# Window attention issued from a job list that a list scheduler in the kernel puts in order

## The chip, the cores and the metric

One core of a Trainium2 chip runs the whole program. The metric is the device time of one execution in microseconds (us); times are medians of several executions on the same chip.

## The reference

```python
scores = scale * np.matmul(q, k.transpose(0, 1, 3, 2))          # q, k, v: 4 x 8 heads x 576 x 64, float32
mask = (rel >= 0) & (rel < window)                              # causal, window = 128
scores = np.where(mask, scores + bias[None], -1000000000.0)     # ALiBi bias
attn = np.exp(scores - np.max(scores, axis=-1, keepdims=True))
x = np.matmul(attn / (np.sum(attn, axis=-1, keepdims=True) + 1e-09), v)   # -> 2304 tokens x 512
h = x @ w_in;  g = h * (1.0 / (1.0 + np.exp(-1.702 * h)));  x = g @ w_out   # first feed-forward net
h = x @ w2_in; g = np.where(h >= 1, h, np.where(h <= -1, 0.0, (h + 1) ** 2 / 4))
out = g @ w2_out                                                # second net; weights are float64
```

## The kernel before

The attention stage comes first; its result stays on chip, transposed, in `xt`. Work is cut into 16 **units** (one batch, two heads). A unit loads q and k (`load_qk`, six DMAs, ten for unit 0) and v (`load_v`, three DMAs), transposes q and k on TensorE in three chunks (`trans_qk`, chunk 2 is 64 rows; its copy out of PSUM is ScalarE's, the others are VectorE's), and makes the scores of five query blocks m = 0 to 4 in three runs (`scores`: m 0 and 1, m 2 and 3, m 4) with 64x64 tiles of the array. VectorE adds the bias and takes the row maximum (L234), ScalarE takes the exponential (L237, nine per unit), VectorE makes the reciprocal of the sums (L245, L246), GpSimd scales (L250). `trans_p` transposes each block of P on TensorE in 128-column chunks, and ScalarE copies it to `pt`: one copy of three chunks for m = 1 to 3 (L265), two copies for the edge blocks m = 0 and 4 (L270 of 64 partitions, L271 of 128). `pv_unit` is 64 matmuls in 64-column tiles into two PSUM buffers of the pool `ps_a`, which `trans_qk` uses too; a ScalarE and a VectorE copy (L294, L295) write `xt`.

Around this, eight half-slices of the first net's weights are converted from float64 in steps (`load_half`: L66 and L76 on ScalarE, L67 to L74 on VectorE, L78 on GpSimd), so that four of sixteen slices lie ready when the first net starts. `split_block` splits `xt` into two float32r parts (L107, L108).

The order of the work is a sorted list of keys: `at(5 * u - 2.87, load_qk, u)` puts the load of unit u at 2.87 fifths of a unit ahead of its scores, and so on. The framework's own scheduler may then still move instructions. Each engine works its queue strictly in the order issued and stops at the first instruction that has to wait. Buffers: q/k raw 3, qk 2, v 2, pt 2, six P buffers; PSUM 2 (`ps_a`), 4 (`ps_s`), 2 (`ps_t`). The two feed-forward nets follow (`ffn`), a dense stream of 128x128 float32r matmuls.

Of the kernel before, what the change touches and what calls it, by code (L numbers as in the profile page):

```python
# [1 line left out]

# [14 lines left out]
SPLIT = 4  # L17
# [5 lines left out]
P = 128  # L23


@with_exitstack
def tile_window_attention_two_ffn(ctx: ExitStack, tc: tile.TileContext, q, k, v, w1_in, w1_out, w2_in, w2_out, out):
# [10 lines left out]
    def f32(ap):  # L38
        return ap.bitcast(F32)
# [18 lines left out]
    def load_half(src, w, i, in_ffn=False):  # L58
        raw = stage.tile([P, 512, 2], I32, tag="raw", name="raw")
        if i == 0:  # L60
            nc.sync.dma_start(out=raw.rearrange("p (c f) t -> p c (f t)", c=KC), in_=src)
        else:
            nc.sync.dma_start(out=raw.rearrange("p f t -> p (f t)"), in_=src)
        lo, hi = raw[:, :, 0], raw[:, :, 1]
        x = stage.tile([P, 512], I32, tag="x", name="x", bufs=2)
        nc.scalar.activation(f32(x), f32(raw)[:, :, 1], AF.Abs)  # L66
        nc.vector.tensor_scalar(  # L67
            out=f32(x), in0=f32(x), scalar1=HI_MIN, scalar2=HI_MAX, op0=ALU.max, op1=ALU.min)
        finish_late()
        nc.vector.tensor_scalar(  # L70
            out=x, in0=x, scalar1=3, scalar2=0x3FFFFFF8, op0=ALU.logical_shift_left, op1=ALU.bitwise_and)
        nc.vector.scalar_tensor_tensor(  # L72
            out=x, in0=lo, scalar=29, in1=x, op0=ALU.logical_shift_right, op1=ALU.bitwise_or)
        nc.vector.scalar_tensor_tensor(  # L74
            out=x, in0=hi, scalar=SIGN_TOP, in1=x, op0=ALU.bitwise_and, op1=ALU.bitwise_or)
        nc.scalar.copy(w[:, 0, i, :], f32(x))  # L76
        if not in_ffn:
            nc.gpsimd.tensor_tensor(out=w[:, 1, i, :], in0=f32(x), in1=f32(w[:, 0, i, :]), op=ALU.subtract)  # L78
            return
        late.append(lambda: nc.vector.tensor_tensor(  # L80
            out=w[:, 1, i, :], in0=f32(x), in1=f32(w[:, 0, i, :]), op=ALU.subtract))

    def load_weights(w_in, w_out, f, w, halves=(0, 1), in_ffn=False):
        for i in halves:
            src = w_out[f * P:(f + 1) * P, :]
            if i == 0:
                src = w_in.rearrange("(c p) f -> p c f", p=P)[:, :, 2 * f * P:2 * (f + 1) * P]
            load_half(src, w, i, in_ffn)
# [5 lines left out]

    def load_w1(f, i):
        if i == 0:
            w1[f] = new_slice(w_a)
        load_weights(w1_in, w1_out, f, w1[f], (i,))
# [14 lines left out]
    with ExitStack() as actx:  # L113
# [9 lines left out]
        ps_a = pool("ps_a", 2, space=PSUM)  # L123
        ps_s = pool("ps_s", 4, space=PSUM)
        ps_t = pool("ps_t", 2, space=PSUM)
# [8 lines left out]
        bias = acon.tile([P, NP, 2, 192], BF16, tag="bias", name="bias")  # L134

        def setup():
            make_identity(nc, ident)
            nc.gpsimd.iota(reli, pattern=[[-1, 256]], base=P, channel_multiplier=1)
# [9 lines left out]
            for j, r in enumerate(HALVES):  # L148
                nc.gpsimd.tensor_copy(band[r, :], mask[r, 64 * j:64 * j + 192])
            for hp in range(NP):  # L150
# [5 lines left out]
        def make_bias(hp):  # L156
            for e in range(2):
                nc.vector.scalar_tensor_tensor(
                    out=bias[:, hp, e, :], in0=rel, scalar=slope[:, hp, e:e + 1], in1=band,
                    op0=ALU.mult, op1=ALU.add)  # L160

        pbuf = [acon.tile([P, 384], F32, tag=f"p{i}", name=f"p{i}") for i in range(6)]
        done = set()

        units = [(b, hp) for b in range(B) for hp in range(NP)]
        NU = len(units)
        NM = 5
        st = [dict() for _ in units]

        def load_qk(u):  # L170
# [16 lines left out]
        def load_v(u):  # L187
# [10 lines left out]
        def trans_qk(u, c):  # L198
# [3 lines left out]
            ps = ps_a.tile([P, 2, 256], F32, tag="a", name="ps_qk")  # L202
            n = 256 if c < 2 else 64
            for i in range(2):
                for t in range(0, n, P):
# [3 lines left out]
                        ident[0:r, 0:r])  # L209
            (nc.scalar.copy if c == 2 else nc.vector.tensor_copy)(  # L210
                d["qk"][:, :, 256 * c:256 * c + n], ps[:, :, 0:n])

        def groups(m):
            return [(e, 2 * m + e, 64 * max(0, 2 - 2 * m - e)) for e in range(2 if m < NM - 1 else 1)]

        def scores(u, ms):
            b, hp = units[u]
            d = st[u]
            ps = [ps_s.tile([P, 2, 256], F32, tag="s", name="ps_s") for _ in range(len(groups(ms[0])))]
            for a, m in enumerate(ms):  # L220
                for e, i, lo in groups(m):
# [5 lines left out]
            sm = d["sm", ms[0]] = st_p.tile([P, 3, 2, 2], F32, tag="sm", name="sm")  # L227
            for a, m in enumerate(ms):
                n = NM * u + m
                assert n < len(pbuf) or n - len(pbuf) in done  # L230
                pt = d["p", m] = pbuf[n % len(pbuf)]
                for e, i, lo in groups(m):
                    x = pt[:, 192 * e + lo:192 * e + 192]
                    nc.vector.tensor_tensor_reduce(  # L234
                        out=x, in0=ps[e][:, a, lo:192], in1=bias[:, hp, e, lo:192], op0=ALU.add, op1=ALU.min,
                        scale=-0.125, scalar=3.0e38, accum_out=sm[:, 0, a, e:e + 1])
                    nc.scalar.activation(  # L237
                        x, x, AF.Exp, bias=sm[:, 0, a, e:e + 1], scale=-1.0, accum_out=sm[:, 1, a, e:e + 1])

        def norm(u, ms):  # L240
            d = st[u]
            sm = d["sm", ms[0]]
            nn = sum(len(groups(m)) for m in ms)
            s = sm.rearrange("p k a e -> p k (a e)")
            nc.vector.tensor_scalar_add(s[:, 2, 0:nn], s[:, 1, 0:nn], 1e-9)  # L245
            nc.vector.reciprocal(s[:, 2, 0:nn], s[:, 2, 0:nn])  # L246
            for a, m in enumerate(ms):
                for e, i, lo in groups(m):
                    x = d["p", m][:, 192 * e + lo:192 * e + 192]
                    nc.gpsimd.tensor_scalar(  # L250
                        out=x, in0=x, scalar1=sm[:, 2, a, e:e + 1], scalar2=1.0, op0=ALU.mult, op1=ALU.mult)

        def trans_p(u, m):
            d = st[u]
            p = d["p", m]
            done.add(NM * u + m)
# [5 lines left out]
            if 0 < m < NM - 1:  # L262
                for c in range(3):
                    nc.tensor.transpose(ps[:, c, :], p[:, 128 * c:128 * c + 128], ident)  # L264
# [236 lines left out]
```

## Time and profile before

| | |
|---|---|
| time, three runs | median 953.44 us (952.15 to 957.61) |
| the profiled execution | 955.39 us, of which its span 953.6 us |
| granted TensorE clock, mean | 0.993 |
| attention stage: start to the first matmul of the nets | 143.55 us |
| PE (TensorE matmul) busy | 933.4 us, 98% of the span |
| DVE (VectorE), ACT (ScalarE), POOL (GpSimd) busy | 542.7, 398.7, 76.7 us |

PEld is the loading of weights into the array, which overlaps with matmuls. Matmuls are pipelined and their ends are modelled, so a busy PE is not PE at its peak. A span in brackets is the idle time before an instruction, with what ended it.

### The profile page before, as it was taken

The numbers are of one execution on the slowest core, as the hardware profiler recorded it, in microseconds if no ns is written. First come the engines' busy times: TensorE is split into PE (matmuls) and PEld (weight loads), VectorE is DVE, ScalarE is ACT, GpSimd is POOL, SyncE is SP. The second block draws the span as 40 slices with busy tenths as digits, with TensorE's granted clock in tenths as the row PEclk, the third lists the DMA queues.
The fourth block names the chain that finished last, engine by engine and source line by source line (L and its number), as shares of the span: only waits on it lengthen the run. The fifth ranks groups of instructions, "written<-read, shape, count | busy, mean of one in ns | idle before, by whom it ended". The sixth has DMA issues, their size and how long they took to land.

```text
span 953.6 us, 15411 instructions
## 1 busy us (share of the span) xinstructions
PE 933.4 (98%) x5904; PEld 816.3 (86%) x5904; DVE 542.7 (57%) x1290; ACT 398.7 (42%) x980; POOL 76.7 (8%) x166
## 2 busy tenths in 40 slices
PE   6999999999999999999999999999999999999998
PEld 3676668889888999998888899989999999999997
DVE  4689868989533323322489899843543544444443
ACT  3799876545323223222344554522322323323322
POOL 3467650000000000000000000000000000000000
PEclk8899999999999999999999999999999999999999
DMA  5578633344200000000034334000000000000000
GB/s 135 119 175 189 161 93 92 131 152 142 96 1 1 1 1 1 1 0 1 1 100 143 111 111 131 36 23 1 34 1 1 34 1 1 34 1 1 34 1 33
DMA packets 83129, 55.31 MB, mean 58 GB/s; under 512 B 59120, under 2 KB 76784, under 8 KB 83056
## 3 DMA queue, kind: packets, MB, share of 16 engines
q1 hardware_dynamic: 82912, 54.21, 19.8%
q8 instruction: 46, 0.75, 0.3%
q14 instruction: 27, 0.22, 0.1%
q10 hardware_dynamic: 144, 0.13, 0.0%
HBM read 48.66 MB, written 5.66 MB: 57 GB/s over the span
## 4 chain that ended last, share of the span: by engine, by line
PE 87%; ACT 4%; DVE 4%; DMA 2%; SPq 1%; issue 1%; POOL 0%; ACTq 0%; POOLq 0%; DVEq 0%
PE ph L350 40%; PE o L413 21%; PE o L411 18%; ACT p L237 3%; PE ps_x L290 3%; PE ps_s L224 2%; PE ps_qk L207 1%; PE ps_t L264 1%; DMA raw<-in_moe_w_out_dram 1%; DMA qkraw<-in_k_dram 1%; DVE x L74 1%; ACT pt L265 1%; DVE x L72 1%; SPq L183 1%; PE ps_t L268 0%
## 5 line engine op out<-in xcount | busy, mean ns | idle before, releaser
L350 PE MATMUL ph<-xs,w 128*128 128x384 f32 (+2 forms) x2112 | 431.1, 353 | 0.0
L350 PEld LDWEIGHTS ph<-xs,w 128*128 128x128 f32 x2112 | 385.2, 188 | 28.6
L413 PE MATMUL o<-w,gs 128*128 128x512 f32 x864 | 215.8, 394 | 0.0
L411 PE MATMUL o<-gs,w 128*128 128x460 f32 (+1 forms) x960 | 214.4, 372 | 0.5 <-DVE gs L364 0.5
L411 PEld LDWEIGHTS o<-gs,w 128*128 128x128 f32 x960 | 180.3, 188 | 21.9 <-DVE gs L364 0.9
L413 PEld LDWEIGHTS o<-w,gs 128*128 128x128 f32 x864 | 161.2, 188 | 30.0 <-ACT gs L363 0.3
L363 ACT CAST gs<-ph 128x384 fp32r<-128x384 f32 (+2 forms) x176 | 89.6, 510 | 164.8 <-DVE ph L361 112.0
L364 DVE TENSOR_TENSOR gs<-ph,gs 128x384 fp32r<-128x384 f32 (+2 forms) x176 | 104.3, 593 | 72.3 <-ACT gs L363 71.5
L360 DVE TENSOR_TENSOR ph<-ph,ga 128x384 f32<-128x384 f32 x96 | 54.2, 566 | 143.6 <-ACT ga L359 143.4
L357 DVE TENSOR_TENSOR ph<-ph,ga 128x460 f32<-128x460 f32 (+1 forms) x80 | 51.4, 643 | 125.5 <-ACT ga L356 125.4
L359 ACT ACTIVATE ga<-ph,half 128x384 f32<-128x384 f32 x96 | 55.8, 582 | 135.3 <-PE ph L350 131.6
L356 ACT ACTIVATE ga<-ph 128x460 f32<-128x460 f32 (+1 forms) x80 | 44.2, 554 | 138.9 <-PE ph L350 138.9
L250 POOL TENSOR_SCALAR p<-p,sm 128x192 f32<-128x192 f32 (+1 forms) x144 | 63.4, 459 | 61.2 <-DVE sm L246 45.1
L237 ACT ACTIVATE p<-p,sm 128x192 f32<-128x192 f32 (+1 forms) x144 | 61.5, 430 | 7.4 <-DVE sm L234 7.0
L66 ACT ACTIVATE x<-raw 128x512 f32<-128x512 f32 x64 | 43.2, 677 | 47.0 <-DMA raw<-in_moe_w_in_dram 22.1
L361 DVE SCALAR_TENSOR_TENSOR ph<-ga,ph 128x384 f32<-128x384 f32 x96 | 53.9, 561 | 2.8
L76 ACT CAST w<-x 128x512 fp32r<-128x512 f32 x64 | 39.3, 617 | 19.5 <-DVE x L74 18.4
L234 DVE CUSTOM_DVE_ANT_0 p<-ps_s,bias 128x192 f32<-128x192 f32 (+1 forms) x144 | 41.6, 329 | 8.4 <-PE ps_s L224 7.6
L74 DVE SCALAR_TENSOR_TENSOR x<-raw,x 128x512 int32<-128x512 int32 x64 | 43.8, 686 | 0.6
L72 DVE SCALAR_TENSOR_TENSOR x<-raw,x 128x512 int32<-128x512 int32 x64 | 43.7, 686 | 0.5
L290 PEld LDWEIGHTS ps_x<-pt,vraw 64*64 64x64 f32 (+1 forms) x1024 | 29.1, 135 | 13.2 <-ACT qk L210 7.3
L290 PE MATMUL ps_x<-pt,vraw 64*64 64x64 f32 (+1 forms) x1024 | 34.6, 227 | 5.5 <-ACT qk L210 5.3
(50 smaller groups left out, 505.6 us busy)
## 6 DMA issues: line engine op xcount, KB each, us to landing
raw<-in_moe_w_in_dram SPq DMA_DIRECT2D x32, 512.0 KB, 3.7
raw<-in_moe_w_out_dram SPq DMA_DIRECT2D x32, 512.0 KB, 3.6
out_dram<-ob SPq DMA_DIRECT2D x17, 256.0 KB, 2.0
vraw<-in_v_dram SPq DMA_DIRECT2D x32, 128.0 KB, 3.2
qkraw<-in_q_dram SPq DMA_DIRECT2D x30, 128.0 KB, 3.5
qkraw<-in_k_dram SPq DMA_DIRECT2D x30, 128.0 KB, 3.4
sp<-part SPq DMA_DIRECT2D x4, 231.0 KB, 3.5
xt<-sp SPq DMA_DIRECT2D x4, 231.0 KB, 3.1
```

The costliest lines, as they stand in the source:

```text
L74: nc.vector.scalar_tensor_tensor(out=x, in0=hi, scalar=SIGN_TOP, in1=x, op0=ALU.bitwise_and, op1=ALU.bitwise_or)
L237: nc.scalar.activation(x, x, AF.Exp, bias=sm[:, 0, a, e:e + 1], scale=-1.0, accum_out=sm[:, 1, a, e:e + 1])
L250: nc.gpsimd.tensor_scalar(out=x, in0=x, scalar1=sm[:, 2, a, e:e + 1], scalar2=1.0, op0=ALU.mult, op1=ALU.mult)
L290: nc.tensor.matmul(x[e][HALVES[j], m, :], vr[rows, kb, HALVES[j]], pt[rows, n, HALVES[j ^ e]], start=(i == first[e]), stop=(i == last[e]), ...
L350: nc.tensor.matmul(ph, w[f][:, a, 0, c * P:(c + 1) * P], xs[r][c][:, b, :], start=(c == 0 and i == 0), stop=(c == KC - 1 and i == 2))
L359: nc.scalar.activation(a, ph, AF.Relu, scale=0.5, bias=half)
L360: nc.vector.tensor_tensor(out=ph, in0=ph, in1=a, op=ALU.max)
L361: nc.vector.scalar_tensor_tensor(out=ph, in0=a, scalar=1.0, in1=ph, op0=ALU.min, op1=ALU.mult)
L363: nc.scalar.copy(gs[:, 0, :], ph)
L364: act_last[0] = nc.vector.tensor_tensor(out=gs[:, 1, :], in0=ph, in1=f32(gs[:, 0, :]), op=ALU.subtract)
L411: nc.tensor.matmul(o[r][m][:, 0:n], w[f][:, a, 1, sl], gs[:, b, :], start=first, stop=last)
L413: nc.tensor.matmul(o[r][m], gs[:, b, sl], w[f][:, a, 1, :], start=first, stop=last)
```

## The change

The attention stage becomes a list of jobs. `jobs` writes down each piece of work with its engine, how long it occupies it, its latency, what it needs, which buffers it takes and gives back, and a key in units. `in_order` runs a list scheduler over them: per engine it looks at the first 12 open jobs in order of key, takes one that can start, preferring a lower key where starts lie within 150 ns, and adds 95 ns where TensorE changes tile shape. The jobs are issued in the order of the resulting starts, under `tc.manual_schedule()`. The steps of a weight half, the bias, the norm and each exponential are jobs of their own. Buffers: raw 4, qk 3, v 3, pt 3, ten P buffers; PSUM as before. For the edge blocks, columns 192 to 255 of each P buffer are cleared once, and two whole 128-column chunks are transposed and copied in one ScalarE copy. The nets' code is the same; their weight conversion keeps its steps.

```diff
+CAPS = dict(raw=4, v=3, qk=3, a=2, s=4, p=10, t=2, pt=3, wraw=2, wx=2)
+KEYS = dict(dma=-3.04, v=-0.71, b=-0.56, q=-0.6, qe=-0.52, s=-0.5, t=-0.3, x=0.08, n=0.67, po=-0.49, pt=0.98, pe=0.72, pv=0.29, xe=0.54)
+STEP, QSTEP, W_AT, W_STEP, XS_AT = 0.243, 0.09, 3.72, 1.69, 28.0
+RUNS = [(0, 1), (2, 3), (4,)]
+SHAPE_SWITCH, SLACK, AHEAD = 95, 150, 12
...
+def jobs(nu, n_heads2, halves, chunks):
...
+            add(("q", u, c), "PE", occ, lat, at("q", c * QSTEP), [("dma", u), ("ident",)] + [("q", u, 0)] * (c > 0),
+                [("a", (u, c))] + [("qk", u)] * (c == 0), [("raw", u)] * (c == 2), "128x128")
...
+                add(("pe", u, m), "ACT", 365 if wide else 260, 510 if wide else 400, at("pe", m * STEP / 2),
+                    [("pt", u, m)], gives=[("t", (u, m))])
+        add(("pv", u), "PE", 1400, 1600, at("pv"), [("dmav", u)] + [("pe", u, m) for m in range(NM)],
+            [("a", (u, 3)), ("a", (u, 4))], [("pt", u), ("v", u)], "64x64")
...
+def in_order(todo, caps):
...
+                t = max([clock[eng]] + [seen[d] for d in j.needs])
+                if j.shape and shape and j.shape != shape:
+                    t = max(t, clock[eng] + SHAPE_SWITCH)
...
+                t = max([t] + [sorted(free[what])[n - 1] for what, n in counts.items()])
+                if first is None or (t <= first[0] + SLACK if j.key < first[1].key else t < first[0] - SLACK):
+                    first = (t, j)
...
-        raw_p = pool("raw_p", 3)
-        qkt_p = pool("qkt_p", 2)
-        v_p = pool("v_p", 2)
-        pt_p = pool("pt_p", 2)
+        raw_p = pool("raw_p", CAPS["raw"])
+        qkt_p = pool("qkt_p", CAPS["qk"])
+        v_p = pool("v_p", CAPS["v"])
+        pt_p = pool("pt_p", CAPS["pt"])
...
+            for p in pbuf:
+                nc.gpsimd.memset(p[:, 192:256], 0.0)
...
-            nc.tensor.transpose(ps[0:64, 1, :], p[:, 128:192], ident)
-            nc.tensor.transpose(ps[:, c, :], p[:, 128 * c:128 * c + 128], ident)
-            nc.scalar.copy(pt[0:64, n + 1, :], ps[0:64, 1, :])
-            nc.scalar.copy(pt[:, n + c, :], ps[:, c, :])
+            for c in chunks_of(m):
+                nc.tensor.transpose(ps[:, c, :], d["p", m][:, P * c:P * c + P], ident)
...
+            nc.scalar.copy(d["pt"][:, 3 * m + c[0]:3 * m + c[-1] + 1, :], d["ps_t", m][:, c[0]:c[-1] + 1, :])
...
-        for key, _, fn, args in sorted(ev, key=lambda e: e[:2]):
-            fn(*args)
-        xs0 = split_block(0, B1[0])
+        with tc.manual_schedule():
+            for _, (what, *args) in in_order(jobs(NU, NP, 2 * SPLIT, KC), CAPS):
+                do[what](*args)
```

What the new order is shows in the built programs. First SP's queue, which issues the loads, at the start (numbers tell units apart). Before, after unit 0's q and k:

```order
L185 DMA qkraw_111<-in_k_dram 64x2x64
L193 DMA vraw_154<-in_v_dram 128x4x64 x2
L195 DMA vraw_154<-in_v_dram 64x2x64
L193 DMA vraw_177<-in_v_dram 128x4x64 x2
L195 DMA vraw_177<-in_v_dram 64x2x64
L183 DMA qkraw_233<-in_q_dram 128x4x64 x2
L185 DMA qkraw_233<-in_q_dram 64x2x64
L183 DMA qkraw_233<-in_k_dram 128x4x64 x2
```

Now:

```order
L317 DMA qkraw_137<-in_k_dram 64x2x64
L315 DMA qkraw_174<-in_q_dram 128x4x64 x2
L317 DMA qkraw_174<-in_q_dram 64x2x64
L315 DMA qkraw_174<-in_k_dram 128x4x64 x2
L317 DMA qkraw_174<-in_k_dram 64x2x64
L315 DMA qkraw_193<-in_q_dram 128x4x64 x2
```

The loads of v of units 0 and 1 stood ahead of unit 1's q and k; they now stand behind the q and k of units 1 and 2.

Then TensorE in the middle of the stage. Before (`ps_s` scores, `ps_qk` 128x64 chunk 2 of q and k, `ps_t` blocks of P, `ps_x` the product with v):

```order
L264 MATMUL ps_t<-ident,p_105 128x128 x3
L207 MATMUL ps_qk<-ident,qkraw 128x128 x3
L224 MATMUL ps_s<-qk 64x64 x2
L224 MATMUL ps_s<-qk 64x128 x2
L224 MATMUL ps_s<-qk 64x192 x4
L264 MATMUL ps_t<-ident,p_106 128x128 x3
L207 MATMUL ps_qk<-ident,qkraw 128x64 x2
L264 MATMUL ps_t<-ident,p_107 128x128 x3
L224 MATMUL ps_s<-qk 64x192 x8
L290 MATMUL ps_x<-pt,vraw 64x64 x32
L268 MATMUL ps_t<-ident,p_108 64x128
L269 MATMUL ps_t<-ident,p_108 128x128
```

Now:

```order
L406 MATMUL ps_t<-ident,p_113 128x128 x3
L406 MATMUL ps_t<-ident,p_114 128x128 x2
L359 MATMUL ps_s<-qk 64x64 x2
L359 MATMUL ps_s<-qk 64x128 x2
L359 MATMUL ps_s<-qk 64x192 x4
L429 MATMUL ps_x<-pt,vraw 64x64 x32
L359 MATMUL ps_s<-qk 64x192 x8
L339 MATMUL ps_qk<-ident,qkraw 128x64 x2
L406 MATMUL ps_t<-ident,p_105 128x128 x2
```

Pieces of one tile shape stand together more often, and here the product with v stands ahead of chunk 2. Over the whole stage TensorE changes between 64-wide tiles (scores and products), the 64-row chunk and the other transposes 133 times before and 95 times now.

Last, VectorE at the end of the stage. Before, from the last score block (`sm_2503`) on:

```order
L234 ISA p1_106,sm_2503<-ps_s_2500,bias_104 128x192
L234 ISA sm_2503 128x1
L245 TENSOR_SCALAR sm_2503<-sm_2503 128x1
L246 RECIPROCAL sm_2503<-sm_2503 128x1
L295 COPY xt2_69<-ps_x_2547 128x4x64
```

Now (`sm_2474`; `x_2531` and `x_2671` are weight halves, the second one of the fifth slice):

```order
L370 ISA p9_114,sm_2474<-ps_s_2473,bias_104 128x192
L370 ISA sm_2474 128x1
L385 TENSOR_SCALAR sm_2381<-sm_2381 128x4
L389 RECIPROCAL sm_2381<-sm_2381 128x4
L199 TENSOR_SCALAR x_2531<-x_2531 128x512
L441 COPY xt2_69<-ps_x_2497 128x4x64
L202 TENSOR_SCALAR x_2531<-x_2531 128x512
L385 TENSOR_SCALAR sm_2474<-sm_2474 128x1
L199 TENSOR_SCALAR x_2671<-x_2671 128x512
L205 SCALAR_TENSOR_TENSOR x_2531<-raw_2100,x_2531 128x512
L389 RECIPROCAL sm_2474<-sm_2474 128x1
```

Between the two steps of the last norm stand two steps of weight conversion.

## Rows read from the trace of the kernel before

**Rows 1.** The page: busy time, share of the span and instructions of each engine.
```profile
PE 933.4 (98%) x5904; PEld 816.3 (86%) x5904; DVE 542.7 (57%) x1290; ACT 398.7 (42%) x980; POOL 76.7 (8%) x166
```
**Rows 2.** Stretches: sum over twelve units, 31.5 to 124.5 us, product to product; busy us.
```profile
sum 93.00, PE 88.22 PEld 64.10 DVE 79.08 ACT 85.16 POOL 57.37; mean PE 7.35 PEld 5.34 DVE 6.59 ACT 7.10 POOL 4.78
```
**Rows 3.** Timeline of PE, attention stage: start, length, instructions merged.
```profile
62.35 0.68 PE L290 MATMUL ps_x<-pt,vraw 128*64 128x64 f32 x14
...
64.65 0.30 PE L268 MATMUL ps_t<-ident,p 128*64 128x128 f32 x1
...
66.17 0.49 PE L264 MATMUL ps_t<-ident,p 128*128 128x128 f32 x3
66.50 0.60 PE L207 MATMUL ps_qk<-ident,qkraw 128*128 128x128 f32 x4
...
68.47 0.55 PE L264 MATMUL ps_t<-ident,p 128*128 128x128 f32 x3
68.95 0.88 PE L224 MATMUL ps_s<-qk 64*64 64x192 f32 x16
69.76 0.34 PE L290 MATMUL ps_x<-pt,vraw 128*64 128x64 f32 x4
...
134.21 2.30 PE L290 MATMUL ps_x<-pt,vraw 128*64 128x64 f32 x64
...
141.74 1.88 PE L290 MATMUL ps_x<-pt,vraw 128*64 128x64 f32 x64
143.55 6.80 PE L350 MATMUL ph<-xs,w 128*128 128x462 f32 x31
```
**Rows 4.** Waits, 32 to 124.5 us: who for whom, us, times, longest.
```profile
ACT p L237 <- DVE sm L234: 4.7, 10, 1.0
PE ps_x L290 <- ACT qk L210: 4.0, 12, 0.7
```
**Rows 5.** Lines of ACT, 31.5 to 124.5 us: busy us, mean ns, idle before.
```profile
L237 ACT ACTIVATE p<-p,sm 128x192 f32<-128x192 f32 (+2 forms) x107 | 45.8, 431 | 5.0 <-DVE sm L234 4.7
...
L66 ACT ACTIVATE x<-raw 128x512 f32<-128x512 f32 x10 | 7.0, 698 | 0.9 <-POOL w L78 0.6 <-DMA raw<-in_moe_w_in_dram 0.2
```
**Rows 6.** Timeline of ACT within one unit.
```profile
65.17 0.42 ACT L294 COPY xt<-ps_x 128x320 f32<-128x320 f32 x1
65.48 0.27 ACT L270 COPY pt<-ps_t 64x128 f32<-64x128 f32 x1
...
65.80 0.64 ACT L76 CAST w<-x 128x512 fp32r<-128x512 f32 x1
66.31 0.47 ACT L237 ACTIVATE p<-p,sm 128x192 f32<-128x192 f32 x1
...
69.72 0.46 ACT L265 COPY pt<-ps_t 128x384 f32<-128x384 f32 x1
70.08 0.26 ACT L210 COPY qk<-ps_qk 128x128 f32<-128x128 f32 x1
70.24 0.48 ACT L265 COPY pt<-ps_t 128x384 f32<-128x384 f32 x1
```
**Rows 7.** Timeline of the start: SP's queue, PE, ACT.
```profile
6.33 1.14 SPq L193 DMA_DIRECT2D vraw<-in_v_dram  x2
...
10.03 1.15 SPq L183 DMA_DIRECT2D qkraw<-in_q_dram  x2
...
16.26 0.66 PE L207 MATMUL ps_qk<-ident,qkraw 128*128 128x128 f32 x2 [1.70 <-DMA qkraw<-in_k_dram]
...
20.24 0.35 ACT L237 ACTIVATE p<-p,sm 128x64 f32<-128x64 f32 x1
...
29.93 0.35 ACT L237 ACTIVATE p<-p,sm 128x64 f32<-128x64 f32 x1 [0.42 <-DVE sm L234]
```
**Rows 8.** Stretches: busy us of PE, PEld, DVE, ACT, POOL; granted clock; DMA.
```profile
16.00:28.00 12.00, 11.60 (x71) 7.35 (x71) 6.15 (x31) 6.12 (x26) 3.57 (x9) 0.50 0.60 135
200.00:240.00 40.00, 40.00 (x193) 36.01 (x193) 38.04 (x70) 20.99 (x38) 0.00 (x0) 1.00 0.43 139
```

More of the change, by code (lines that the diff above doesn't have):

```diff
@@ L1 @@
+from collections import Counter, namedtuple
 from contextlib import ExitStack, nullcontext
+from functools import partial
 import numpy as np
@@ new lines, in in_order @@
+def in_order(todo, caps):
+    queues = {}
+    for j in sorted(todo, key=lambda j: j.key):
+        queues.setdefault(j.eng, []).append(j)
+    clock = dict.fromkeys(queues, 0)
+    free = {what: [0] * n for what, n in caps.items()}
+    seen, shape, order = {}, None, []
+    while any(queues.values()):
+        best = None
+        for eng, queue in queues.items():
+            first = None
+            for j in queue[:AHEAD]:
+                if any(d not in seen for d in j.needs):
+                    continue
+                t = max([clock[eng]] + [seen[d] for d in j.needs])
+                if j.shape and shape and j.shape != shape:
+                    t = max(t, clock[eng] + SHAPE_SWITCH)
+                counts = Counter(what for what, _ in j.takes)
+                if any(len(free[what]) < n for what, n in counts.items()):
+                    continue
+                t = max([t] + [sorted(free[what])[n - 1] for what, n in counts.items()])
+                if first is None or (t <= first[0] + SLACK if j.key < first[1].key else t < first[0] - SLACK):
+                    first = (t, j)
+            if first and (best is None or first[0] < best[0]):
+                best = first
+        t, j = best
+        queues[j.eng].remove(j)
+        clock[j.eng] = t + j.occ
+        seen[j.name] = t + j.lat
+        shape = j.shape or shape
+        for what, _ in j.takes:
+            free[what].sort()
+            free[what].pop(0)
+        for what, _ in j.gives:
+            free[what].append(t + j.lat)
+        order.append((t, j.name))
+    return order
@@ L56, in finish_late, with load_raw @@
             late.pop()()
-    def load_half(src, w, i, in_ffn=False):
+    def load_raw(w_in, w_out, f, i):
         raw = stage.tile([P, 512, 2], I32, tag="raw", name="raw")
         if i == 0:
+            src = w_in.rearrange("(c p) f -> p c f", p=P)[:, :, 2 * f * P:2 * (f + 1) * P]
             nc.sync.dma_start(out=raw.rearrange("p (c f) t -> p c (f t)", c=KC), in_=src)
         else:
[L63 to L81, printed above, removed]
@@ L90, in new_slice, with load_weights @@
+    def load_weights(w_in, w_out, f, w):
+        for i in range(2):
+            raw = load_raw(w_in, w_out, f, i)
+            x = stage.tile([P, 512], I32, tag="x", name="x", bufs=2)
+            for step in range(6):
+                convert(step, raw, x, w, i, nc.vector)
+                if step == 1:
+                    finish_late()
+            late.append(partial(convert, 6, raw, x, w, i, nc.vector))
     def new_slice(pool):
@@ L154, in setup, with do_b, do_dma @@
                         nc.vector.memset(slope[r, hp, e:e + 1], -8.0 * 2.0 ** (-8.0 * (h + 1) / H))
[L156 to L170, printed above, removed]
+        def do_b(hp, e):
+            nc.vector.scalar_tensor_tensor(
+                out=bias[:, hp, e, :], in0=rel, scalar=slope[:, hp, e:e + 1], in1=band, op0=ALU.mult, op1=ALU.add)
+        def do_dma(u):
             b, hp = units[u]
@@ L275, in pv_unit, with do_pv @@
+        def do_pv(u):
             d = st[u]
             pt, vr = d["pt"], d["v"]
-            x = [ps_a.tile([P, 8, 64], F32, tag="a", name="ps_x") for _ in range(2)]
+            x = d["ps_x"] = [ps_a.tile([P, 8, 64], F32, tag="a", name="ps_x") for _ in range(2)]
             todo = []
```

266 lines of the change are left out of this document (175 added, 91 removed).

## The prediction

> **What bounds the kernel now.** The page comes first: PE is busy 98% of the span [rows 1], so whatever the change gives must come out of time in which PE is busy with little or waits. The timeline of PE then shows where the change can act at all. The attention stage runs until the nets' first matmul at 143.55 us [rows 3]; behind that the nets' code and order are the same. So the question is how much earlier that matmul starts.
>
> Inside the stage I read the period of a unit, from one product with v to the next. It is 69.76 - 62.35 = 7.41 us in one of the tightest units, and (134.21 - 31.5) / 13 = 7.90 us as the mean of thirteen [rows 2, 3]: 31.5 is the start of the stretch of rows 2, 134.21 that of a later product. Of twelve units' 93.0 us PE is busy in 88.22 and ACT in 85.16, DVE in 79.08, POOL in 57.37 [rows 2]. Two engines are close to full, and each waits now and then for the other: each product with v waits for ACT's copy of chunk 2 (12 waits, 4.0 us), ACT's exponentials for DVE (4.7 us) [rows 4]. A stage of that sort is bound by neither engine alone but by both and the order in which they meet.
>
> What each engine needs without waits is the floor. **PE:** a product takes 143.55 - 141.74 = 1.81 us when nothing holds it, and 64.65 - 62.35 = 2.30 us in the unit read [rows 3]; without these 0.49 us the unit has 7.41 - 0.49 = 6.92 us of PE work. **ACT:** nine exponentials at 0.431 us, 3.88 [rows 5]; the wide copy 70.08 - 69.72 = 0.36, three of them 1.08; chunk 2, 70.24 - 70.08 = 0.16; the xt copy 65.48 - 65.17 = 0.31; a pair of edge copies 65.80 - 65.48 = 0.32, two pairs 0.64 [rows 6]. Together 6.07 us a unit, without weights. A weight half adds 0.698 (L66) [rows 5] and 66.31 - 65.80 = 0.51 (L76) [rows 6], 1.21 us; eight of them, spread over 16 units, are 0.60 a unit. So ACT has 6.67 us of work in 7.90, PE 6.92; the mean unit waits about 0.98 us on PE.
>
> **The change part by part.**
>
> *Edge copies.* Of each pair one copy of 256 columns remains. 128 columns take 0.16 and 384 take 0.36 [rows 6], so 256 take 0.26: 0.06 saved per pair, 0.12 a unit. ACT's floor falls to 6.55 us. The transposes stay as many; the ten memsets of P buffers lie on POOL ahead of its first scaling, which waits for the first exponentials anyway; if that cover failed they would delay unit 0 alone.
>
> *Order on PE.* There are 38 fewer changes of tile shape. A row of three transposes takes 66.50 - 66.17 = 0.33 us when transposes follow, and 68.95 - 68.47 = 0.48 us when scores follow [rows 3]: 0.15 us for a change. 38 x 0.15 = 5.7 us, 0.36 a unit: PE's floor falls from 6.92 to 6.56 us. I take no more, since the two ends of such a step are alike elsewhere; nothing if the wait were there for another reason.
>
> *Order and deeper buffers together.* Both floors are then near 6.56 us, against a period of 7.90. No row of the old trace shows what the new order leaves in waits. The bounds: none (6.56), or all of today's loss kept (7.90). I take the middle of today's 0.98 us of waits, 0.49, since some of it is of a kind that the new order removes (in the place shown, the product no longer has chunk 2 ahead of it) while each engine still stops at its first waiting instruction: 6.56 + 0.49 = 7.05 us. 13 units x (7.90 - 7.05) = **11.0 us less**.
>
> *Start.* The six DMAs of v for units 0 and 1 occupy SP's queue from 6.33 to 10.03 us [rows 7], ahead of unit 1's q and k. They now come later, so unit 1's last k lands 3.7 us earlier: its transposes, which waited for k until 16.26 [rows 7], can start at 12.56. From there to unit 1's first exponential it was 20.24 - 16.26 = 3.98 us [rows 7]; kept, it starts at 16.5. Up to unit 2's first exponential ACT has by its new order nine exponentials, unit 0's five copies and one chunk 2: 3.88 + 1.08 + 0.52 + 0.16 = 5.64 us, so 22.2. Before it was 29.93 [rows 7], with two copies more done (0.32 + 0.36). **Gain 29.93 - 0.68 - 22.2 = 7.0 us.** The difference to the bare 3.7 us is that PE ran this stretch at a granted clock of 0.50 [rows 8], the 1.2 GHz level, after it had waited for q and k; with the loads 3.7 us earlier the wait is short. Bounds: 3.7 us if the clock still falls, 8.5 us if at 2.4 GHz the 3.98 us shrink to 2.5 too (an estimate: PE's part of it at half length).
>
> SP's queue later: q and k are issued three units ahead, v about two, and a load of v waits for the product three units back with the next q and k queued behind it. With four raw buffers that is 2 units or 14 us of room, so I cost it at nothing; were v late by more, PE would wait for k.
>
> *End.* The last reciprocal stands behind two weight steps on DVE, the first of which waits for an L66 on ACT, and the last copies to pt behind split casts (four, moved here from units 1 to 4, whose 2 us then fall out of the units' periods) and one weight cast. From the rows, between 0 (hidden) and three steps of 0.7 [rows 5]; I take **1.0 us more**, since the chain from the last exponential to the nets is a serial one.
>
> **The sum:** -7.0 - 11.0 + 1.0 = **-17.0 us**. Against the profiled execution, 955.39 - 17.0 = 938.4 (span 936.6); that run lies 1.95 us over the median of the runs, 953.44, so the time I forecast is **936.4 us**. The nets' first matmul would stand at about 126.5.
>
> **The rivals.**
>
> *A, the floor is reached:* 13 x (7.90 - 6.56) = 17.4, start 8.5, end 0: -25.9, **927.5 us**. For it: buffers for a unit more everywhere, and an order made with latencies. Against: two engines equally full, in strict order.
>
> *B, PE is as full as it looks.* If its busy time is real, the units can give no more than PE's idle time, 93.00 - 88.22 = 4.78 us in twelve [rows 2], 5.2 in thirteen: -7.0 - 5.2 + 1.0, **942.2 us**. Against it: the weight loads fill only 64.10 of the 93.00 us [rows 2], and 6.92 us of work in 7.90 were found. The Trainium skill, page "Perfetto Trace Analysis", section "Identifying the Most-Contended Engine", says that matmul busy time is no good measure of TensorE's room and the busy share of LDWEIGHTS is: by it 69% here, room for A or the forecast, by the other 95% and B.
>
> *C, the waits only change their names.* PSUM is as scarce as before (2, 4 and 2 banks), and the wait that repeats in every unit is for a PSUM buffer of `ps_a` [rows 4]. Then the units keep 7.90 us: -7.0 + 1.0, **947.4 us**. The Trainium skill, the same page, section "Optimization Strategy", says that a gap that repeats on the full engine can mean too few SBUF or PSUM buffers; here only SBUF gets more, which by that sentence alone speaks for C.
>
> *D, the clock falls at the start all the same:* -3.7 - 11.0 + 1.0, **939.7 us**; with C together 950.7 us.
>
> *E, slower: ACT stands at each copy of P.* ACT's new order has five copies to pt a unit, fixed between exponentials by the scheduler's own figures, which price a product at 1.4 us where 1.81 is measured and a change of shape at 0.095 where it is 0.15. If PE is late, ACT stops at the copy with ready exponentials queued behind it, and these feed the scaling and so the next transposes. At worst each of the five waits for its transposes' 0.55 us [rows 3]: 6.55 + 2.75 = 9.30 us a unit, 13 x 1.40 = 18.2 more, less 6.0 from start and end: +12.2, **965.6 us**. It decides once ACT's waits pass 7.90 + 6.0 / 13 - 6.55 = 1.8 us a unit. Against it: pt is three deep now and PE's floor no higher than ACT's.
>
> *F, the nets give some back:* DVE is busy 38.04 of 40 us in their opening [rows 8], converting weights, and the new order leaves about one half-slice more to do then, some four steps of 0.7 us [rows 5]: up to 2.8 us of PE's time if nothing covers them, 939.2 us with the forecast's other terms, inside its range.
>
> **How the numbers follow.** Forecast 52% (931 to 942), A 10%, B 13%, C 6%, D 10%, C with D 5%, E 4%. The range of 8 in 10 goes from the floor to C: **927 to 948 us**. A measurement of this kernel can tell about 0.5%, 4.8 us, from no change: faster than 948.6 are the forecast, A, B, C and D, 0.91; within it C with D, 0.05; slower 0.04.
>
> **What would show it.** Right: the nets' first matmul at 124 to 130 us; a mean period near 7.05 between products (they come less evenly, so over ten or more); unit 2's first exponential near 22 us and a granted clock of 1.0 in 16 to 28; no wait of PE on chunk 2 in every unit; PE's busy time still above 90%. Wrong: the period at 7.6 or more with waits of ACT on `ps_t` (E or C), a clock of 0.5 past 20 us (D), or PE waiting inside the nets (F).

## The result, and the profile after

The changed kernel takes 945.56 us (median of four runs, 944.14 to 946.71) against 955.53 us for the kernel before, run beside it on the same chip: a ratio of 0.9896, 95% interval 0.9855 to 0.9938. It is faster by 10.0 us; forecast was 17.0 us. The profiled spans say the same, 953.6 and 943.6 us. The time lies inside the range of the prediction, but the terms of its sum miss by 2 to 6 us each, so each is taken by itself.

The page's line of engines, which answers to [rows 1], tells nothing: PE is as full as before.

```profile
PE 921.8 (98%) x5904; PEld 810.7 (86%) x5904; DVE 546.8 (58%) x1290; ACT 398.2 (42%) x948; POOL 76.7 (8%) x176
```

Four marks cut the program into four stretches: unit 2's first exponential, unit 15's first exponential, the nets' first matmul, the end. An exponential is a better mark than a product with v here, since the new order issues products unevenly. Three rows of the timeline of the changed kernel (start us, length, engine, line, operation):

```profile
20.54 0.35 ACT L378 ACTIVATE p<-p,sm 128x64 f32<-128x64 f32 x1
...
118.23 0.35 ACT L378 ACTIVATE p<-p,sm 128x64 f32<-128x64 f32 x1
...
131.54 0.47 PE L497 MATMUL ph<-xs,w 128*128 128x462 f32 x1
```

In the kernel before the same marks stand at 29.93 [rows 7], 133.07 and 143.55 us [rows 3]. The period below is the time from the first mark to the second, divided by 13.

| stretch | before | after | gain | forecast |
|---|---|---|---|---|
| start, to unit 2's first exponential | 29.93 | 20.54 | 9.4 | 7.0 |
| units 2 to 15, 13 periods | 7.93 each | 7.51 each | 5.4 | 11.0 |
| end, to the nets' first matmul | 10.48 | 13.31 | -2.8 | -1.0 |
| nets | 810.05 | 812.06 | -2.0 | 0 |
| sum | 953.6 | 943.6 | 10.0 | 17.0 |

The stretches of the changed kernel (start:end and length; busy us of PE, PEld, DVE, ACT, POOL with counts; granted clock; DMA share; GB/s) show the start and the nets at once:

```profile
16.00:28.00 12.00, 11.85 (x192) 8.86 (x192) 10.76 (x56) 11.37 (x46) 7.45 (x19) 1.00 0.66 148
31.00:116.00 85.00, 77.28 (x1317) 57.20 (x1316) 71.19 (x325) 76.33 (x294) 49.87 (x106) 1.00 0.71 168
131.00:160.00 29.00, 29.00 (x168) 26.03 (x164) 26.11 (x47) 16.53 (x29) 1.11 (x1) 1.00 0.38 124
160.00:200.00 40.00, 37.75 (x177) 32.77 (x176) 37.09 (x70) 20.54 (x39) 0.00 (x0) 1.00 0.47 144
```

How the 12.0 us ahead of the nets divide among the first three stretches depends on the marks. When unit 2's exponentials begin, the new kernel already runs unit 0's product, the old one has not begun it, so that the 13 periods hold 12 products now and 13 before. By products, the forecast's own mark, the first, the fourteenth and the last stand here:

```profile
31.49 0.34 PE L290 MATMUL ps_x<-pt,vraw 128*64 128x64 f32 x4
19.54 1.81 PE L429 MATMUL ps_x<-pt,vraw 128*64 128x64 f32 x61
...
118.78 1.88 PE L429 MATMUL ps_x<-pt,vraw 128*64 128x64 f32 x64 [0.26 <-DVE xt L441]
...
129.72 1.89 PE L429 MATMUL ps_x<-pt,vraw 128*64 128x64 f32 x64
```

The first row is of the kernel before, the others are of the changed one. The start then gains 31.49 - 19.54 = 12.0 us; the 13 periods behind the first product go from 7.90 to (118.78 - 19.54) / 13 = 7.63 us, 3.5 us less in all; and the last two periods of products lose as much. From the first product to the last it is 110.2 us before and now.

From 16 to 28 us the granted clock is 1.00 where it was 0.50 [rows 8], and PE passes 192 matmuls where it passed 71. From 160 to 200 us PE has 2.25 us without work; in the kernel before it was busy for 39.97 of these 40. The waits of PE say where that is. First those from 31 to 124 us (who for whom: us in total, times, longest), then those behind 131.5 us:

```profile
PE ps_s L359 <- DVE qk L345: 2.5, 3, 0.9
PE ps_t L406 <- POOL p L394: 2.3, 5, 0.7
PE ps_t L406 <- ACT pt L411: 1.3, 3, 0.6
PE ps_x L429 <- DVE xt L441: 0.9, 2, 0.6
PE ps_qk L339 <- DMA qkraw<-in_k_dram: 0.6, 1, 0.6
...
PE o L558 <- DVE part L522: 1.8, 3, 0.6
PE o L558 <- ACT gs L510: 0.5, 1, 0.5
```

The wait of every product for chunk 2 (12 times, 4.0 us [rows 4]) is gone, and 8.0 us of waits under other names have come, of which the five largest are shown. In the nets PE waits for `part`, DVE's copies of a partial sum to be spilled; in the kernel before it had no such wait.

The end is read from DVE's timeline, with PE's last transposes behind it:

```profile
126.76 0.14 DVE L385 TENSOR_SCALAR sm<-sm 128x1 f32<-128x1 f32 x1
126.82 0.58 DVE L199 TENSOR_SCALAR x<-x 128x512 f32<-128x512 f32 x1
127.33 0.68 DVE L205 SCALAR_TENSOR_TENSOR x<-raw,x 128x512 int32<-128x512 int32 x1
127.93 0.14 DVE L389 RECIPROCAL sm<-sm 128x1 f32<-128x1 f32 x1
...
129.35 0.44 PE L406 MATMUL ps_t<-ident,p 128*128 128x128 f32 x2 [0.64 <-POOL p L394]
```

The reciprocal of the last group of rows, 0.14 us of work, starts 1.17 us after its sum, behind two weight steps; the scaling, the last transposes and the last product follow in a chain. That is the term "End", seen as forecast, though at 2.8 us in place of 1.0.

### The profile page after: what moved, and what is told of

The parts are those of the page before. It is cut to its first block, busy times and chain, and to the rows that moved or that the text cites. A ratio compares the mean times of both kernels' runs of the same rounds, so it can differ in the third digit from the quotient of the medians.

```text
span 943.6 us, 15391 instructions
## 1 busy us (share of the span) xinstructions
PE 921.8 (98%) x5904; PEld 810.7 (86%) x5904; DVE 546.8 (58%) x1290; ACT 398.2 (42%) x948; POOL 76.7 (8%) x176
## 4 chain that ended last, share of the span: by engine, by line
PE 85%; DVE 6%; DMA 4%; ACT 2%; SPq 1%; issue 1%; POOL 0%; ACTq 0%; DVEq 0%; POOLq 0%
PE ph L497 39%; PE o L560 21%; PE o L558 19%; PE ps_x L429 2%; DMA raw<-in_moe_w_in_dram 2%; PE ps_s L359 2%; DMA raw<-in_moe_w_out_dram 1%; PE ps_t L406 1%; PE ps_qk L339 1%; DVE x L208 1%; DVE x L205 1%; DVE p L370 1%; DMA qkraw<-in_k_dram 1%; DVE qk L345 1%; DMA sp<-part 1%
## 5 line engine op out<-in xcount | busy, mean ns | idle before, releaser
L406 PE MATMUL ps_t<-ident,p 128*128 128x128 f32 x208 | 36.7, 288 | 5.5 <-POOL p L394 3.9
L213 DVE TENSOR_TENSOR w<-x,w 128x512 fp32r<-128x512 f32 x56 | 38.3, 687 | 2.2 <-ACT w L211 0.6
```

## The experiments

Times are medians, unless a single run is named. Ratios are to the kernel before, on the same chip. The changed kernel's own stage, which stands unchanged up to the last unit in three of the runs below (10 to 12), has periods of 7.54 to 7.60 us there against 7.51, so differences below 0.1 us a period mean nothing. The granted clock has to be read beside the period: from 31 to 116 us it is 1.00 in the change, and 0.88 to 0.98 in all of the runs 3 to 12 but the one with both reliefs (7): PE had stood somewhere in its units, and 0.50 was granted for some microseconds behind it.

### 1. The loads alone, in the old order

```
-        load_v(0)
+        at(-9.2, load_v, 0)
...
-                at(5 * u - 2.87, load_qk, u)
+                at(5 * u - 2.87 if u > 1 else -9.5, load_qk, u)
```

> The kernel before, with unit 1's q and k issued ahead of the v loads of units 0 and 1, and nothing else. Theory: the start's gain is the loads' alone and needs no new order. Unit 2's first exponential moves from 29.93 us to between 21 and 23, the granted clock stays at 1.0 between 16 and 28 us, the units behind keep their 7.93 us, and the kernel becomes 7 to 9 us faster. Rival: the start needs the new order too, since unit 0 and unit 1 are still issued as before; then unit 2's first exponential stays above 25 us and no more than 4 us are gained. Second rival: the clock falls all the same, with a wait one unit later; gain 3.7 us.

Measured: 949.0 us, ratio 0.9934 (0.9913 to 0.9954), 6.7 us less; span 947.9. The timeline of ACT and the stretch from 16 to 28 us:

```profile
22.29 0.35 ACT L237 ACTIVATE p<-p,sm 128x64 f32<-128x64 f32 x1 [0.36 <-DVE sm L234]
```
```profile
16.00:28.00 12.00, 11.58 (x159) 7.65 (x158) 8.44 (x48) 11.18 (x49) 6.39 (x18) 1.00 0.62 139
```

Unit 2's first exponential comes 7.6 us earlier and the clock does not fall: most of the start's gain is the loads' (by products 7.1 of 12.0 us, with unit 0's at 24.41). Behind it the period is 8.03, the end 10.48 us, so 5.7 us of span remain, a little under what was expected. Of the change's 10.0 us more than half is six DMA issues moved.

### 2. Loads, whole edge blocks and deeper buffers, in the old order

```
-        raw_p = pool("raw_p", 3)
+        raw_p = pool("raw_p", 4)
...
-            nc.scalar.copy(pt[0:64, n + 1, :], ps[0:64, 1, :])
-            nc.scalar.copy(pt[:, n + c, :], ps[:, c, :])
+            nc.scalar.copy(pt[:, n + lo:n + lo + 2, :], ps[:, lo:lo + 2, :])
```

(and qk, v and pt to 3, P to ten buffers, the loads as in 1).

> The kernel before with the loads moved, the edge blocks copied whole and all the deeper buffers (raw 4, qk 3, v 3, pt 3, ten P buffers), in the old order. Theory: buffers alone change nothing, since a written order stops at the same instruction whatever lies free; the edge copies give at most 0.12 us a unit. So 0 to 2 us faster than with the loads alone, period 7.8 to 7.93. Rival: the old order waits for buffers, and the depth alone gives a good part of what the change gave in its units (0.42 us each): 4 us or more over the loads alone, period 7.6 or less.

Measured: 954.97 us, ratio 0.9997 (0.9975 to 1.002). Neither theory: 6 us slower than the loads alone. The waits of PE from 10 to 35 us show why at the start:

```profile
PE ps_qk L211 <- DMA qkraw<-in_k_dram: 0.9, 1, 0.9
PE ps_qk L211 <- DMA qkraw<-in_q_dram: 0.8, 1, 0.8
```

On SP's queue unit 2's v now stands ahead of its q and k (issued at 13.70 and from 15.55 us), which a third v buffer allows, and the first mark moves from 22.29 to 23.71 us. The period is 7.98, so the buffers and the edge copies together do not shorten the units in the old order, and the end grows to 14.95 us, where PE waits 1.84 us in the middle of a product and then runs at a granted clock of 0.84 (131 to 160 us). By the medians the changed kernel, with the new order, is 9.4 us faster than this one; the two were not run side by side, and by the profiles 3.2 us of it is this kernel's later start and 1.6 its longer end. The edge copies were not tried alone; whatever they give is hidden in 7.98.

### 3. Six P buffers in the new order

```
-CAPS = dict(raw=4, v=3, qk=3, a=2, s=4, p=10, t=2, pt=3, wraw=2, wx=2)
+CAPS = dict(raw=4, v=3, qk=3, a=2, s=4, p=6, t=2, pt=3, wraw=2, wx=2)
```

> The changed kernel with six P buffers as before instead of ten, in its pool and in the scheduler's list. Theory: P's buffers are the one depth that the new order lives on, since its exponentials run a unit ahead of the transposes; with six the order falls back to at least the old period, 7.9 us or more, and the kernel to 955 us or more. Rival: the order makes the gain and the depth only follows; period 7.6 or less.

Measured, a single run: 979.85 us, period 9.64. (The scheduler counts free P buffers but does not name them. With six, twelve query blocks lose their buffer to a new block before they are transposed, so part of the attention output is wrong.) This does not show the depth by itself. The scheduler makes another order with six, some transposes now stand behind the scores and exponentials of the block that took the buffer (2.0 us of PE's waits from 24 to 150 us, and none in the change), PE stops more often and the granted clock from 31 to 116 us is 0.88. What is shown is that this scheduler with these keys makes no usable order from six; that P's depth is of no use to the old order fits experiment 2, where it was one of several changes. The Trainium skill, page "Perfetto Trace Analysis", section "Optimization Strategy", says that a gap which repeats can mean too few SBUF or PSUM buffers; this run, 2.1 us a unit longer with six P buffers, fits that and cannot tell it from the changed order.

### 4. Truer prices for PE

```
-        add(("pv", u), "PE", 1400, 1600, at("pv"), [("dmav", u)] + [("pe", u, m) for m in range(NM)],
+        add(("pv", u), "PE", 1650, 1850, at("pv"), [("dmav", u)] + [("pe", u, m) for m in range(NM)],
-SHAPE_SWITCH, SLACK, AHEAD = 95, 150, 12
+SHAPE_SWITCH, SLACK, AHEAD = 200, 150, 12
```

> The changed kernel with the scheduler's prices of a product at 1.65 us instead of 1.4 and of a change of tile shape at 0.2 us instead of 0.095, both nearer to the trace; the order changes, the work does not. Theory E': the mispriced PE is why waits of 0.7 us a unit were left; with true prices the copies of P come in their places, the period falls to 7.2 or less and the kernel is 3 to 5 us faster than the change. Rival, theory P: the waits are small beside PE's own work and another order of the same work gives the same period, 7.4 to 7.6, within 1.5 us of the change.

Measured: 955.12 us, ratio 1.0006 (0.999 to 1.0023); period 8.32. (Here too, for two query blocks P is overwritten before it is transposed.) Unit 1's product comes at 44.85 us instead of 27.62, and from 20 to 60 us PE waits 3.7 us for q and k. Neither theory came. The new order puts products off, unit 1's first, and makes them up in two places: the time from first exponential to first exponential is 15.99 us from unit 5 to 6 and 14.22 from 13 to 14, with a granted clock of 0.50 from 41.5 to 51.7 and from 109.7 to 116.6 us, where PE had stopped (the profile is of the fastest of ten runs). The whole is worse with these keys; how much of it is the order and how much the clock was not separated, and whether mispriced PE left the waits (E') stays open.

### 5. No weight steps among the units; 6. less work in the product; 7. both

```
-STEP, QSTEP, W_AT, W_STEP, XS_AT = 0.243, 0.09, 3.72, 1.69, 28.0
+STEP, QSTEP, W_AT, W_STEP, XS_AT = 0.243, 0.09, 30.0, 1.69, 28.0
```
```
+            todo = todo[:9]
             first = [min(i for i, t in enumerate(todo) if t[0] == e) for e in range(2)]
```

The first diff alone:

> The changed kernel with the eight weight halves planned behind all units, so that ACT, DVE and POOL have no weight steps among them; the whole is longer, since the nets then wait for weights. Read is the period of a unit (first exponential of unit 2 to that of unit 15, divided by 13: 7.51 us in the change). Theory Q: PE stands because ACT and DVE deliver late, and their weight steps (1.21 us on ACT and some 2.2 on DVE for each half) take the time; the period falls to 7.1 or less. Theory P: PE's own work with its shape changes is what fills the unit (6.83 us busy in the new trace and more than my floor of 6.56); the period stays at 7.3 or more.

The second alone:

> The changed kernel with 9 of the 16 groups of matmuls in each product with v; the seven groups over the middle block of keys are left out (all but the first query group's), so part of the attention output is missing. PE has 7/16 of 1.65 us, about 0.72 us, less to do in each unit, ACT, DVE and POOL exactly as much as before. Theory P (PE's own work fills the unit): the period falls from 7.51 us by most of the 0.72, to 7.0 or less. Theory Q (ACT and DVE with their weight steps set the pace): the period stays above 7.3 and PE's idle time grows by what it was spared.

Both:

> Both reliefs at once: no weight steps among the units (ACT is spared 0.6 us a unit, DVE 1.1) and 9 of 16 groups of matmuls in each product (PE is spared 0.72; part of the attention output is missing). Alone the first gave a period of 7.41 and the second 7.36, against 7.51. Theory T, two engines that are both near full and meet in a fixed order: relieved together they give about the 0.6 us that neither gave alone, period 6.9 or less. Theory U, order, transfers and buffers set the period and the engines' work does not: 7.2 or more.

Measured, a single run each: 966.35, 943.15 and 961.61 us, of which only the units count. Periods: **7.41** without weight steps, **7.36** with less product, **6.79** with both (first exponentials at 20.72 and 108.97 us). The stretch from 31 to 116 us of the three, in that order:

```profile
31.00:116.00 85.00, 80.40 (x1404) 61.26 (x1402) 57.76 (x311) 72.74 (x290) 39.81 (x103) 0.98 0.58 135
```
```profile
31.00:116.00 85.00, 76.71 (x1070) 55.78 (x1072) 72.33 (x327) 77.05 (x299) 50.89 (x106) 0.96 0.73 171
```
```profile
31.00:116.00 85.00, 80.10 (x1186) 59.13 (x1184) 60.50 (x330) 78.85 (x317) 44.61 (x116) 1.00 0.58 133
```

Relieving ACT (with DVE and POOL) gives 0.10 us a unit, relieving PE by 0.72 gives 0.15, both together 0.72. But the three did not run at the same granted clock: 0.98, 0.96 and 1.00 in these rows. Each single relief has one unit, from first exponential to first exponential, that is longer than the same one of the change: without weight steps the one from 76.94 to 87.78 us, 10.84 us for 8.50; with less product the one from 34.51 to 44.85 us, 10.34 for 8.79. PE stops in each, and the clock falls behind the stop. Without weight steps:

```profile
78.55 2.42 PE L429 MATMUL ps_x<-pt,vraw 128*64 128x64 f32 x61 [2.14 <-DMA vraw<-in_v_dram]
80.00:84.00 4.00, 4.00 (x58) 3.16 (x56) 1.70 (x10) 1.48 (x5) 0.42 (x1) 0.57 0.69 156
```

With less product:

```profile
41.42 0.39 PE L339 MATMUL ps_qk<-ident,qkraw 64*128 64x64 f32 x2 [1.73 <-DVE xt L442]
41.00:45.00 4.00, 3.58 (x17) 2.59 (x18) 3.83 (x21) 3.54 (x14) 0.82 (x2) 0.57 0.74 166
```

Without that one unit, in the run and in the change alike, the two reliefs give 0.31 and 0.29 us a unit, 0.60 together, and both at once 0.72. So P and Q fall, each by the run in which it asked for 7.0 or 7.1: neither side alone sets the pace. T's number came, 6.79, but that the two together give what neither gives alone is not shown; they may simply add, and the stops and the clock that they bring take a part (theory U), as the wait for v here. Each of the three is one profile.

The rows also show what PE's busy time is worth. With less product PE does 0.72 us less in each unit, yet its busy time goes only from 77.28 / 85 x 7.51 = 6.83 to 76.71 / 85 x 7.36 = 6.64 us a unit. That is not the clock alone: from 66 to 116 us, at 1.00 in the change (first row) and with less product (second), it goes from 45.58 / 50 x 7.42 = 6.76 to 45.27 / 50 x 7.20 = 6.52, with the periods of units 8 to 15.

```profile
66.00:116.00 50.00, 45.58 (x780) 33.96 (x778) 42.46 (x195) 45.95 (x178) 31.40 (x64) 1.00 0.68 163
66.00:116.00 50.00, 45.27 (x663) 32.83 (x659) 43.61 (x196) 47.06 (x183) 32.18 (x63) 1.00 0.67 161
```

### 8. Weight loads earlier on SP's queue

```
+def early_loads(order):
+    for h in range(8):
+        i = order.index(("wd", h))
+        before = [j for j in range(i) if order[j][0] in ("dma", "dmav")][-3:]
+        j = max([before[0]] + [order.index(("w4", g)) + 1 for g in [h - 2] if g >= 0])
+        order.insert(j, order.pop(i))
+    return order
```

> The changed kernel with each weight half's load issued three loads earlier on SP's queue and not a row moved on the other engines. In the new trace SP issues without a pause from 49.5 to 75 us and ACT stands 2.9 us at L197 for two weight loads that come late, with exponentials queued behind. Theory S: late transfers take a part of the units; ACT's waits there vanish and the period falls from 7.51 to about 7.3, 2 to 3 us faster than the change. Rival: the time is lost at the next wait instead (q and k then come later by one load, PE waits for k); the period stays within 0.1 us and the time within 1 us of the change's.

Measured: 946.55 us, ratio 0.9915 (0.9886 to 0.9944); period 7.68. ACT's waits for weights are gone, and among PE's waits from 21 to 117 us stands now

```profile
PE ps_qk L348 <- DMA qkraw<-in_k_dram: 1.8, 1, 1.8
```

where it was 0.6 us. The rival's mechanism came: PE waits for k instead. Its time came too, 1.0 us over the change, but not its period, which is 0.17 us longer. That is one unit, from 34.32 to 46.18 us, 11.86 us for 8.79, with the wait for k (36.42 us) and a granted clock of 0.50 behind it from 38.1 to 41.5; the other twelve are 0.07 us shorter on the mean.

### 9. Weight steps and split casts earlier

```
-STEP, QSTEP, W_AT, W_STEP, XS_AT = 0.243, 0.09, 3.72, 1.69, 28.0
+STEP, QSTEP, W_AT, W_STEP, XS_AT = 0.243, 0.09, 3.72, 1.45, 9.0
```

> The changed kernel with the weight halves planned 1.45 instead of 1.69 units apart and the four split casts planned from unit 9 on instead of behind everything. In the new trace the last unit's reciprocal stands 1.2 us behind two weight steps on DVE, and two weight steps on ACT stand ahead of the last exponential. Theory: the stretch from the last unit's first exponential to the nets, 13.3 us now and 10.5 in the kernel before, falls to 11.5 or less, and the units get longer by no more than 0.1 us, since PE fills them: 0.5 to 2.5 us faster than the change. Rival: ACT and DVE set the pace of the units, so that what is taken from the end comes back there, 8 casts of some 0.5 us; within 0.5 us of the change.

Measured: 949.32 us, ratio 0.9938 (0.9919 to 0.9958). The kernel is 3.8 us slower than the change, so neither theory nor rival came. The end falls to 11.91 us, most of the way to the 11.5 expected, and the nets to 809.1, but the period rises to 8.19, 8.8 us in all, for eight split steps of some 0.5 to 0.7 us and one weight half. The order changed everywhere else too, and the granted clock from 31 to 116 us is 0.96; how much is due to each stays open.

### 10. The last weight half behind the last scalings

```
+def late_steps(order):
+    last = [n for n in order if n[0] in ("w0", "w1", "w2", "w3", "w4", "w5", "w6") and n[1] == 7]
+    order = [n for n in order if n not in last]
+    i = order.index(("po", 15, 2, 4, 0)) + 1
+    return order[:i] + last + order[i:]
```

> The changed kernel with the seven steps of the last weight half issued behind the last unit's scalings instead of among its exponentials and reciprocal, all else in the same order. Theory: in the last 13.3 us the serial chain from the last exponential to the nets is held by these steps (0.57 us on ACT ahead of the last exponential, 1.2 us on DVE ahead of the last reciprocal), so the stretch falls to about 12.0 and the kernel is 1.0 to 1.7 us faster than the change. Rival: the weights then come late in the nets, whose DVE is full at their opening, and PE waits there for what was gained here; within 0.5 us of the change.

Measured: 949.63 us, ratio 0.9951 (0.9931 to 0.9971), 4.1 us slower than the change. The end grew to 16.72 us. ACT and PE there (line numbers are 7 higher than the change's):

```profile
132.75 0.62 ACT L218 CAST w<-x 128x512 fp32r<-128x512 f32 x1 [2.26 <-DVE x L215]
133.27 0.57 ACT L466 CAST xs<-xt 128x462 fp32r<-128x462 f32 x1
133.75 0.36 ACT L418 COPY pt<-ps_t 128x256 f32<-128x256 f32 x1
```
```profile
134.16 1.74 PE L436 MATMUL ps_x<-pt,vraw 128*64 128x64 f32 x36 [3.68 <-ACT pt L418]
```

The reciprocal came at once (0.18 us after its sum), but the steps now stood ahead of the last copy to `pt` on ACT: a cast that waited 2.26 us for DVE held it, and PE stood 3.68 us. It is rival E's mechanism, ACT standing in strict order ahead of a copy that PE needs, in one place; the edit was a step short.

### 11. `part` on ACT

```
-                    nc.vector.tensor_copy(part, src[:, 0:n])
+                    nc.scalar.copy(part, src[:, 0:n])
```

> The changed kernel with the four copies of a partial sum to `part` in the first net on ACT instead of DVE. Theory: the 2.0 us that the nets gave back are PE's waits for these copies, because DVE comes to them late with conversions ahead of them; then PE's idle time between 160 and 200 us goes from 2.25 us to under 0.7 and the kernel is about 1.5 to 2 us faster than the change. Rival: it is the conversions themselves that are late, or the spill's transfers that hold the buffer; then PE waits as long behind another name and the time stays within 0.5 us of the change's.

Measured: 943.38 us, ratio 0.9886 (0.9843 to 0.9929). The stretch from 160 to 200 us:

```profile
160.00:200.00 40.00, 39.47 (x189) 35.16 (x189) 36.46 (x67) 21.75 (x41) 0.00 (x0) 1.00 0.48 155
```

PE has 0.53 us without work there instead of 2.25, and the nets take 942.3 - 132.32 = 810.0 us as in the kernel before. The nets' loss was these copies on a late DVE.

### 12. Both ends together

`part` on ACT, and `late_steps` with the steps behind the last copy to `pt` and the split casts:

```
-    i = order.index(("po", 15, 2, 4, 0)) + 1
+    i = max(order.index(("pe", 15, 4)), order.index(("xl", 3))) + 1
```

> The changed kernel with two edits: the copies to `part` on ACT (2.2 us by the run that had it alone), and the seven steps of the last weight half issued behind the last unit's copies of P and the split casts, not among its exponentials and not, as in the run that lost 3.4 us, ahead of its last copy. Theory: the last reciprocal and the last copy both come at once, the stretch from the last unit's first exponential to the nets falls from 13.3 to 11.8 to 12.3 us, the nets take 810 us, and the kernel is 3 to 3.7 us faster than the change, about 942. Rival: DVE, full at the nets' opening, now has seven steps more to do there, PE waits for it at the hidden layer, and only the 2 us of the first edit remain or less: 943.5 to 945.

Measured: 944.63 us, ratio 0.9896 (0.9876 to 0.9917). The end is 12.12 us, 1.2 less, as expected; but the nets take 811.7 us. PE's waits from 110 to 400 us begin with

```profile
PE ph L504 <- ACT w L218: 1.7, 2, 1.6
```

The rival held: the weight steps pushed behind the stage are late for the nets. Of all kernels that do the whole work, the one of experiment 11 has the lowest median, 2.2 us under the change's; the two intervals overlap, and what speaks for it is the 2.1 us that the nets' stretch lost.

## Why the prediction was right or wrong

**Right: the bound, as far as tried.** "Bound by neither engine alone" is what experiments 5 to 7 show. "The order in which they meet" as the rest of it is argued: the changed order moved the waits and did not shorten them.

**Wrong: the size of the units' gain, -11.0 against -5.4 us.** The step that failed is "I take the middle of today's 0.98 us of waits". By the forecast's floors the new order kept all of that loss. With the forecast's floors the period lies 7.93 - 6.92 = 1.01 us over the higher floor before, and 7.51 - 6.56 = 0.95 after; in experiments 5 to 7, with ACT's floor at 5.95 or PE's at 5.84 or both, it lies 0.85, 0.81 and 0.84 over, though the first two hold a unit at a lowered clock, and 0.56 and 0.57 without it. So the loss was kept from the kernel before to the change, and the gain, 0.42 us a unit, is about the floor's fall, 0.36. By products the period is 7.63 us, 1.07 over the floor and a gain of 0.27, which is no better; the nets' first matmul, at 131.54 us, missed the forecast's 124 to 130. The upper bound was set wrong with it: "all of today's loss kept" is 6.56 + 0.98 = 7.54 us, not 7.90. That the floor falls by 38 changes of shape at 0.15 us fits this, but was not tried by itself, and why the loss stays about 1 us is open.

**Edge copies and depth.** 0.12 us a unit for the copies was never seen apart. Deeper buffers give the old order nothing (2); that P's are needed by the new one is likely and not shown apart from the order (3); the depth of raw, qk, v and pt was not tried alone in it.

**Start, -7.0 against -9.4.** The mechanism was right: loads earlier, short wait, clock at 2.4 GHz. Unit 1's transposes start at 11.85 us, where 12.56 was forecast, and from unit 1's first exponential to unit 2's it is 20.54 - 14.86 = 5.68 us, where 5.64 was. The mis-sized term is the one between, 3.98 us "kept": it is 14.86 - 11.85 = 3.01, as only the bound of 8.5 had it. That the old order with the loads moved reaches 22.29, where 22.2 was forecast, is luck: there unit 1's first exponential is earlier (15.60 for 16.5) and the way to unit 2's longer (6.69 for 5.64).

**End, +1.0 against +2.8.** The mechanism was right and undersized: the last reciprocal stands 1.17 us behind its sum. Moving the last half's steps gave 1.2 of it back (12). The rest was not taken apart.

**The rivals.** A did not come. B's number for the units (5.2 us) is close to the 5.4 measured, yet that is luck, for its reason falls: with 0.72 us less work PE's busy time shrank by a third of that or less, so a good part of it was not work. The Trainium skill, page "Perfetto Trace Analysis", section "Identifying the Most-Contended Engine", says that matmul busy time is no good measure of how full TensorE is; the run agrees, 0.24 us of 0.72 at a granted clock of 1.00. C, the waits change names, is half of the truth: the names changed and the loss of about 1 us a unit stayed, while the floor moved under it. Whether PSUM is behind that loss was not tried. D did not come: the clock stayed at 1.00 in the start. E did not come in the units: ACT waits 3.8 us for copies in 93, not 1.8 a unit. **F came**, 2.0 us of its 2.8, by copies that stood behind conversions; the forecast had it inside its range and left it out of its sum.

## What to carry to other kernels

Where two engines are both near full and meet in strict order, work out each floor, and add the loss that the kernel already shows over the higher one, in full, unless something shows that it goes: here the new order moved the waits and removed none on the whole. Before crediting a reordering, look for the moved DMA issue at its start; here that was over half of the gain. To tell a bound by one engine from a bound by two, relieve each alone and then both, and read the period, not the busy time, and only where the granted clock is the same. A stretch between two marks gains or loses by what the new order moves across a mark, so read a second pair of marks too.

## Not expected of the hardware

TensorE's busy time is elastic: with 0.72 us a unit less to do it fell by 0.24 at a granted clock of 1.00 (experiment 6). And a single stop in one unit can take most of what a relief gives: behind waits of 2.14 and 1.73 us in experiments 5 and 6 the clock stood at 0.50 for some 3.4 us, and the unit took 1.5 to 2.3 us more than in the change; behind a wait of 0.82 us, at 45.24 us in the change, it stayed at 1.00. With both reliefs PE waited for weights at the nets' start, was busy for 8.24 of the 15 us from 116 to 131, and 0.77 was granted there. The same stage code ran at 1.00 in one profile and at 0.98 in three others, with periods 0.03 to 0.09 us longer.
